# Moving the first loads, sums and norms of a fused attention and feed-forward kernel between queues and places

## The chip, the cores and the metric

The kernel runs on one core of a Trainium2 chip. The core has five engines with an instruction stream each: TensorE (PE, matmuls; PEld is its loading of weights), VectorE (DVE), ScalarE (ACT), GpSimd (POOL) and SyncE (SP). Engines wait for one another through semaphores; each works off its own stream in order. Sixteen DMA engines move data. SP and ACT give them transfers through hardware queues (q1 and q10 in the profile), POOL through a software queue (q0), which can also convert types on the way. The metric is the device time of one execution in microseconds (us). The median of three runs before the change is 415.71 us (415.38 to 417.54).

## What is computed

Attention by cosine similarity over 8 batches of 12 heads, 448 tokens, 64 columns a head, and then a feed-forward layer over the 3584 tokens of all batches, all arrays float32:

```python
q_n = q / (np.linalg.norm(q, axis=-1, keepdims=True) + 1e-06)
k_n = k / (np.linalg.norm(k, axis=-1, keepdims=True) + 1e-06)
scores = np.matmul(q_n, k_n.transpose(0, 1, 3, 2)) / tau        # tau = 0.1
scores = scores - np.max(scores, axis=-1, keepdims=True)
attn = np.exp(scores)
attn = attn / (np.sum(attn, axis=-1, keepdims=True) + 1e-09)
x = np.matmul(attn, v)              # to (3584, 768), heads side by side
h = x @ w_in                        # 768 x 2048
out = np.maximum(0.01 * h, h) @ w_out   # 2048 x 768
```

## The kernel before

Heads go in pairs: a *slot* s is one pair of one batch, six slots to a batch (0 to 5 are the first batch), 48 in all. The 448 tokens of a head are three times 128 tokens (the *main* part) and 64 more (the *remainder*). Two slots make a *group* j (j = 0, 1, 2 for the first batch), whose products with v are taken together.

For each slot the steps are these. `load_first` (slots 0 to 5, line 124) or `load_qk` (from 6 on, line 139) brings q and k; the remainders of q and k of a slot share one row of the tile and are transfers of their own. `squares` (line 175) squares both on POOL (slots 0 and 1 on ACT and DVE). `sums` (line 188) adds them on DVE, in two parts. `roots` (line 199) takes the root on ACT as Exp of half a Ln. `normalise` (line 209) divides on DVE and gives qn. `transposes` (line 245) gives qkT: for slots 0 to 9 on TensorE, with a copy out of PSUM by DVE, from slot 10 on by a DMA transpose that SP issues (line 251). `scores` (line 261) multiplies, and ACT takes Exp (line 288). For a group, `totals` (line 323) sums the weights, `products` (line 335, matmuls at line 316) multiplies with v_b and v_rem, the main part and the remainder of v, and `scale` (line 346, DVE) writes xT. Then `first` (line 365, matmuls at line 374) multiplies xT with w_in, and `two_groups` (line 432, matmuls at line 453) with w_out.

The weights come as bfloat16 through POOL's queue: w_in in four transfers (`load_w_in(0)` to `(3)`, 768 KB each in bfloat16), w_out in five. `load_w_in(0)` and `(1)` are the first half of the columns, even and odd rows. `load_v(j)` brings v_b of a group, 192 KB, by the same queue, and `load_v_rem(b)` the remainders of a batch in four small ones. POOL must issue all these between its squares. `hold` (line 508) is a one-element copy on POOL that makes POOL wait until a given value exists.

The order on each engine is that of the program, written out by hand. Ahead of the loop stand the first loads (lines 471 to 478), slot 0, and the beginnings of slot 1 (lines 517 to 550). The loop over the six first slots (line 553) is staged: turn s takes the scores of slot s, norm s+1 with its transposes, sums s+2 and squares s+3, and every second turn the products of a group two slots back. A transfer of SP waits until the one eight places back on the hardware queues has landed.

After the loop come the products of group 2 (`attend(NQ - 1)`, line 702) and the first feed-forward stage of the first batch. From there each batch has the same turn: `visit` (scores of the next batch between the matmuls of w_out, line 677), `attend_batch` (totals and products, line 648), and `firsts` (the matmuls of w_in, line 667), which runs functions of a list `between` ahead of its m-th block of columns. `norm(s)` (line 653) is roots, normalise, transposes, a load_qk of a later slot, hold and squares of slot s+2. `visit` begins with two score tiles that need qkT of the first four slots of the next batch, so of slots 12 to 15 in the visit that ends the turn `b == 0`.

These lines carry the staging of the loop:

```python
scores(s, (1,))
fill(2)                      # matmuls on a constant tile
if s and n:
    sums(n, (0,))            # n = s + 2
if s < 5:
    normalise(s + 1)
```

Of the kernel before, what the change touches and what calls it, by code (L numbers as in the profile page):

```python
# [16 lines left out]
def kernel(  # L17
# [49 lines left out]
    gp = nc.gpsimd  # L67
# [36 lines left out]
    def load_w_in(i):  # L104
        n0, e = i // 2 * (D_ff // 2), i % 2
        gp.dma_start(
            out=w_in_sb[:, e::2, n0 : n0 + D_ff // 2], in_=w_in_r[e, :, :, n0 : n0 + D_ff // 2]
        )
# [15 lines left out]
    def load_first(eng, x, part, s0, n):  # L124

        h0, i = 2 * s0, 0 if x is q else 1
        if part == 0:
            dst = raw0[:, s0 : s0 + n, :, 4 * i : 4 * i + 3]
            eng.dma_start(
                out=dst.rearrange("p s h t d -> p (s h) t d"), in_=main(x, 0, h0, 2 * n)  # L130
            )
        else:
            dst = raw0[64 * i : 64 * i + 64, s0 : s0 + n, :, 3]
            eng.dma_start(
                out=dst.rearrange("p s h d -> p (s h) d"),
                in_=x[0, h0 : h0 + 2 * n, MAIN:S].rearrange("h p d -> p h d"),
            )

    def load_qk(s):
        if s >= NSLOT:  # L140
            return
        b, h0 = s // NPAIR, 2 * (s % NPAIR)
        both = ldp.tile([128, 2, 7, D], F32, name="qk")
        nc.sync.dma_start(out=both[:, :, 0:3], in_=main(q, b, h0, 2))
        nc.sync.dma_start(out=both[:, :, 4:7], in_=main(k, b, h0, 2))
        for i, x in enumerate((q, k)):
            nc.sync.dma_start(
                out=both[64 * i : 64 * i + 64, :, 3],
                in_=x[b, h0 : h0 + 2, MAIN:S].rearrange("h p d -> p h d"),
            )  # L150
        raw[s] = (both[:, :, 0:4], both[:, :, 4:7])
# [5 lines left out]
    def load_v(j):  # L157
        if j >= B * NQ:
            return
        b, jj = divmod(j, NQ)  # L160
        vb[j] = vbp.tile([128, 4, 3, D], BF16, name="v_b")
        gp.dma_start(out=vb[j], in_=main(v, b, 4 * jj, 4))  # L162

    def load_v_rem(b, parts=slice(0, 4)):
        if b >= B:
            return
        x = vrb[b % 2].rearrange("p j g d -> p (j g) d")
        for lo, h0, h1 in ((0, 0, 2), (64, 2, 6), (0, 6, 10), (64, 10, 12))[parts]:
            gp.dma_start(  # L169
                out=x[lo : lo + 64, h0:h1], in_=v[b, h0:h1, MAIN:S].rearrange("h p d -> p h d")  # L170
            )
# [16 lines left out]
    def sums(s, parts=(0, 1)):  # L188
        if s >= NSLOT:
            return  # L190
        if s not in ss:
            ss[s] = smp.tile([128, 14], F32, name="ss")
        for i in parts:
            o = ss[s][:, 0:8] if i == 0 else ss[s][:, 8:14]
            nc.vector.tensor_reduce(  # L195
                o.rearrange("p (h t) -> p h t", h=2), sqs[s][i], axis=AX.X, op=ALU.add
            )

    def roots(s):
        if s >= NSLOT:  # L200
            return
        nc.scalar.activation(ss[s], ss[s], func=AF.Ln, bias=tiny)
        nc.scalar.activation(ss[s], ss[s], func=AF.Exp, scale=0.5)  # L203
        if s < 2:
            nc.scalar.activation(ss[s], ss[s], func=AF.Identity, bias=eps)
# [55 lines left out]
    def scores(s, kis):  # L261
        key_tiles([(s, ki) for ki in kis])
# [210 lines left out]
        load_first(nc.scalar, k, part, 0, 1)  # L473
    load_first(nc.sync, q, 0, 1, 1)
    load_first(nc.scalar, k, 0, 1, 1)
    for part, s, n in ((1, 1, 1), (0, 2, 1), (0, 3, 1), (0, 4, 2)):
        for x in (q, k):
            load_first(nc.sync, x, part, s, n)
    tiny = cpool.tile([128, 1], F32, name="tiny")
# [28 lines left out]
    def hold(x):  # L508
        seen = smp.tile([128, 1], F32, name="seen")
        gp.tensor_copy(out=seen, in_=x)  # L510

    hold(raw0[:, 0, 0, 3, 0:1])
    for x in (q, k):
        load_first(gp, x, 1, 2, 4)
    load_v_rem(0, slice(0, 2))


    (q_h, k_h), (q_h1, k_h1) = raw[0], raw[1]
# [14 lines left out]
    nc.scalar.activation(sqs[1][0], q_h1, func=AF.Square)  # L533
    normalise(0)
    load_qk(6)
    hold(qn[0][:, 6, 0, 0:1])
    squares(2)
    load_w_in(0)
    load_v(0)
    dst = qtp.tile([128, 7, 128], BF16, name="qkT")  # L540
    qkT[0] = dst.rearrange("p t c -> p (t c)")
    for lo, hi, copy in ((0, 4, nc.scalar.copy), (4, 7, nc.vector.tensor_copy)):
# [4 lines left out]
        copy(out=dst[:, lo:hi], in_=tp[:, lo:hi])  # L547
    fill(3)
    sums(1, (0,))
    roots(1)  # L550


    for s in range(NPAIR):
        j = s // 2 - 1 if s >= 2 else None
        even = s % 2 == 0
        n = s + 2 if s + 2 < NPAIR else None
        if s != 3 and s != 5:
            scores(s, (0,))
        if s == 1:
            roots(2)  # L560
        if j is not None and not even:
            products(j, 1)
        scores(s, (1,))
        fill(2)
        if s and n:
            sums(n, (0,))
        if s < 5:
            normalise(s + 1)
            if s != 1 and s < 4:
                load_qk(s + 7 - (s > 1))  # L570
        if j is not None and not even:
            scale(j, 0)
        if s < 5:
            hold(qn[s + 1][:, 6, 0, 0:1])
            squares(s + 3)
        if s == 0:
            load_v_rem(0, slice(2, 4))
        if s in (1, 2):
            load_w_in(s)
        if s < 2:  # L580
            load_v(s + 1)
        elif s == 2:
            load_w_in(3)
        elif s == 3:
            load_w_out(0)
        elif s == 4:
            load_w_out(1, 4)
        if n:
            sums(n, (1,))
        scores(s, (2,))  # L590
        if s == 5:

            scale(j, 1)
            for m in range(SOON):
                pms[0, m] = banks(1, (0, m, 0), 4 + m)
            first(0, 0, range(KT - 2))
        elif not even:
            fill(2)
        if not even:
            scores(s, (3,))  # L600
        if s < 5:
            transposes(s + 1)
        if s == 0:
            sums(2, (0,))
        if s == 5:
            first(0, 1, range(KT - 2))
            sums(6)
            sums(7)
        elif not even:
            fill(2)  # L610
        if n and s:
            roots(n)
        if j is not None and not even and s < 5:
            scale(j, 1)
        if j is not None and even:
            totals(j)
            scores(s + 1, (0,))
            products(j, 0)

    def attend(j, behind=()):  # L620
        totals(j)
        po = banks(2)
        for e in range(2):
            products(j, e, po[:, e])
        for fn in behind:
            fn()
        for e in range(2):
            scale(j, e)
# [17 lines left out]
                scale(j, e)  # L646

    def attend_batch(b):
        attend_two(b * NQ)
        attend(b * NQ + 2)  # L650


# [64 lines left out]
    for b in range(B):  # L717
        tokens = chunk_cols(b)[1] // 128
        if b == B - 1:
            for ts in range(tokens):  # L720
                for half in range(2):
                    second(b, ts, half)
            break
        order = [((ts, 0), (ts, 1)) for ts in range(tokens)]
        if b == 0:
            order = [((0, 0), (1, 0)), ((2, 0), (0, 1)), ((1, 1), (2, 1))]
        visit(b, order, tokens - 1, three if tokens == 3 else four)
        ready += tokens - 1
        attend_batch(b + 1)
        for j in range((b + 2) * NQ, (b + 3) * NQ):  # L730
            load_v(j)
        load_v_rem(b + 2)
        s = ready
        between = {0: [lambda s=s: norm(s)], 1: [lambda s=s: sums(s + 1)]}
        if b == 0:
            between = {
                0: [lambda: load_qk(14), lambda: load_qk(15), lambda: sums(12)],
                1: [lambda: norm(12), lambda: sums(13)], 4: [lambda: norm(13), lambda: sums(14)],
                7: [lambda: norm(14), lambda: sums(15)], 9: [lambda: norm(15)],
                13: [lambda: sums(16)],  # L740
            }
            ready += 4
        elif tokens == 3:
            between.update({
                4: [lambda s=s: norm(s + 1), lambda s=s: sums(s + 2)],
                7: [lambda s=s: norm(s + 2), lambda s=s: sums(s + 3)],
                10: [lambda s=s: norm(s + 3)], 13: [lambda s=s: sums(s + 4)],
            })
            ready += 4
        else:  # L750
            between.update({
                4: [lambda s=s: norm(s + 1)], 5: [lambda s=s: sums(s + 2)],
                8: [lambda s=s: norm(s + 2)], 12: [lambda s=s: sums(s + 3)],
            })
            ready += 3
        firsts(b + 1, 0, between)
# [35 lines left out]
```

## Time and profile before

| | |
|---|---|
| median of three runs | 415.71 us |
| the profiled execution: its time, its span | 416.25 us, 414.5 us |
| busy: PE, ACT, DVE, POOL | 400.8, 260.2, 191.6, 140.4 us |
| moved by DMA | 54.21 MB |
| DMA queues, share of 16 engines | q1 42.3%, q0 22.8% |
| PE L374 (w_in), PE L453 (w_out) | 147.3, 142.7 us |
| PE L316 (totals and products with v) | 32.0 us |

A row of the timeline reads: start and busy time in us, engine, line, operation, the tile written and the tile read, their shapes, how many in a row, and in brackets how long the engine stood idle before and what ended that. A row of waits has the total time, how often, and the longest. In the DMA answers a row names the transfer and the issuing queue, the size, and the time from issue to landing. Rows of windows have, after the stretch and its length, the busy time of PE, PEld, DVE, ACT and POOL with their instructions, the granted clock of TensorE (1.00 is full), the share of DMA time and GB/s. Landing times that the text gives are the issue plus the time to landing.

### The profile page before, as it was taken

How to read it: one execution, taken by the hardware profiler on the slowest of the kernel's cores; microseconds unless marked ns; L12 is line 12 of the kernel's file. 1: busy time of each engine (PE TensorE's matmuls, PEld its weight loads, DVE VectorE, ACT ScalarE, POOL GpSimd, SP SyncE). 2: the span in 40 equal slices, each digit the busy share in tenths (PEclk: the TensorE clock that was granted, in tenths of full speed). 3: DMA queues.
4: the chain of work that ended last, by engine and by line, in shares of the span. 5: the costliest groups of instructions: out<-in, count | busy, mean ns of one | idle time of the engine just before them, and what ended most of it. 6: DMA issues, size and time to landing. Idle time of an engine off the chain costs nothing.

```text
span 414.5 us, 10095 instructions
## 1 busy us (share of the span) xinstructions
PE 400.8 (97%) x4088; PEld 213.3 (51%) x4099; DVE 191.6 (46%) x412; ACT 260.2 (63%) x448; POOL 140.4 (34%) x214
## 2 busy tenths in 40 slices
PE   8589999999899999999999999999999999999996
PEld 3134655544455555544555555544555565544564
DVE  5575863366453625257261735156362554140021
ACT  4688579745785469745775559855776559934300
POOL 3794453535140624055231533153232530000000
PEclk9899999999999999999999999999999999999999
DMA  6999999686585956476476875576377853210023
GB/s 177 243 213 207 214 159 210 170 150 144 132 183 109 131 138 141 128 113 131 96 188 132 108 174 111 121 115 151 89 180 155 110 90 61 63 40 2 0 76 78
DMA packets 103871, 54.21 MB, mean 131 GB/s; under 512 B 69712, under 2 KB 98768, under 8 KB 103824
## 3 DMA queue, kind: packets, MB, share of 16 engines
q1 hardware_dynamic: 77776, 40.98, 42.3%
q0 software_dynamic: 25200, 12.06, 22.8%
q8 instruction: 32, 0.52, 0.6%
q10 hardware_dynamic: 848, 0.52, 0.4%
q14 instruction: 15, 0.12, 0.1%
HBM read 45.61 MB, written 11.01 MB: 137 GB/s over the span
## 4 chain that ended last, share of the span: by engine, by line
PE 92%; DMA 3%; POOL 2%; issue 1%; ACT 1%; DVE 0%; POOLq 0%
PE ps L374 35%; PE ps L453 30%; PE ps L316 12%; PE ps L276 8%; PE ps L411 5%; PE ps L303 1%; DMA raw<-in_q_dram 1%; POOL sq L184 1%; DMA raw<-in_k_dram 1%; DMA qkT<-qn 1%; ACT pe L288 1%; PE ps L233 1%; POOL v_rem L169 0%; DVE qn L219 0%; POOL v_b L162 0%
## 5 line engine op out<-in xcount | busy, mean ns | idle before, releaser
L374 PE MATMUL ps<-xT,w_in_sb 128*128 128x384 bf16 (+1 forms) x760 | 147.3, 352 | 0.4
L453 PE MATMUL ps<-w_out_sb,hT 64*128 64x384 bf16 x1536 | 142.7, 323 | 0.0
L288 ACT ACTIVATE pe<-ps 128x896 bf16<-128x896 f32 x144 | 123.6, 918 | 23.1 <-PE ps L276 21.1
L381 ACT ACTIVATE hT<-ps 128x384 bf16<-128x384 f32 (+1 forms) x128 | 67.5, 543 | 70.5 <-PE ps L374 70.0
L374 PEld LDWEIGHTS <-w_in_sb 128*128 128x128 bf16 x768 | 74.1, 98 | 71.3 <-issue 3.4
L453 PEld LDWEIGHTS <-hT 64*128 64x128 bf16 x1536 | 73.6, 94 | 54.8 <-issue 3.2
L184 POOL TENSOR_TENSOR sq<-qk 128x512 f32<-128x512 f32 x84 | 77.2, 939 | 13.8 <-DMA qk<-in_k_dram 12.6
L276 PE MATMUL ps<-qkT 64*128 64x448 bf16 (+1 forms) x384 | 54.6, 357 | 6.5 <-DVE qkT L257 3.5
L463 DVE COPY osb<-ps 128x384 f32<-128x384 f32 x48 | 24.5, 552 | 78.0 <-PE ps L453 44.9
L195 DVE TENSOR_REDUCE ss<-sq 128x6 f32<-128x384 f32 (+1 forms) x95 | 54.5, 610 | 4.6 <-POOL sq L184 4.4
L510 POOL CAST seen<-qn 128x1 f32<-128x1 bf16 x48 | 9.1, 189 | 130.1 <-DVE qn L219 123.9
L219 DVE TENSOR_TENSOR qn<-qk,r 128x512 bf16<-128x512 f32 x84 | 49.8, 634 | 2.0 <-DMA qk<-in_k_dram 0.3
L214 DVE TENSOR_SCALAR ss<-ss 128x14 f32<-128x14 f32 x46 | 9.3, 202 | 66.0 <-ACT ss L203 66.0
L351 DVE TENSOR_TENSOR xT<-ps,rb 128x448 bf16<-128x448 f32 x48 | 27.7, 619 | 23.4 <-ACT rb L330 23.3
L162 POOL DMA_DIRECT2D v_b<-in_v_dram x24 | 18.5, 773 | 59.1 <-PE ps L316 59.1
L316 PE MATMUL ps<-pe,v_b 128*32 128x448 bf16 x576 | 32.0, 353 | 0.0
L276 PEld LDWEIGHTS <-qkT 64*128 64x128 bf16 (+1 forms) x384 | 16.6, 97 | 27.5 <-issue 11.0
L329 ACT ACTIVATE rb<-ps 128x448 f32<-128x448 f32 x24 | 13.0, 540 | 23.3 <-PE ps L316 23.3
L288 ACT ACTIVATE pr<-ps 128x896 bf16<-128x896 f32 x24 | 21.4, 921 | 0.6 <-PE ps L276 0.5
L417 DVE COPY osb<-ps 128x384 f32<-128x384 f32 (+1 forms) x9 | 4.6, 512 | 36.6 <-issue 22.6
L316 PEld LDWEIGHTS <-v_b 128*32 128x32 bf16 x576 | 15.3, 97 | 11.9 <-DMA v_b<-in_v_dram 0.3
L411 PE MATMUL ps<-w_out_sb,hT 128*128 128x384 bf16 (+1 forms) x144 | 21.0, 308 | 0.0
(51 smaller groups left out, 196.7 us busy)
## 6 DMA issues: line engine op xcount, KB each, us to landing
qk<-in_q_dram SPq DMA_DIRECT2D x42, 192.0 KB, 3.1
qk<-in_k_dram SPq DMA_DIRECT2D x42, 192.0 KB, 3.1
out_dram<-osb SPq DMA_DIRECT2D x30, 192.0 KB, 3.0
v_b<-in_v_dram POOLq DMA_DIRECT2D x24, 192.0 KB, 4.8
out_dram<-osb SPq DMA_DIRECT2D x12, 384.0 KB, 2.7
w_in_sb<-in_moe_w_in_dram POOLq DMA_DIRECT2D x4, 768.0 KB, 11.8
w_out_sb<-in_moe_w_out_dram POOLq DMA_DIRECT2D x1, 1536.0 KB, 21.7
w_out_sb<-in_moe_w_out_dram POOLq DMA_DIRECT2D x4, 384.0 KB, 22.6
```

Source lines behind the costliest of these rows:

```text
L184: eng.tensor_tensor(sq, x, x, op=ALU.mult)
L195: nc.vector.tensor_reduce(o.rearrange("p (h t) -> p h t", h=2), sqs[s][i], axis=AX.X, op=ALU.add)
L219: nc.vector.tensor_tensor(qn[s][:, lo:hi], x.rearrange("p h t d -> p t h d"), r[:, r0 : r0 + 2 * nt].rearrange("p (h t) -> p t h", h=2) .u ...
L276: nc.tensor.matmul(out=out[:, a, :S], lhsT=x[rows, c0:c1], rhs=x[rows, 0:S], start=True, stop=True,)
L288: nc.scalar.activation(out=dst, in_=sc[:, :, :S], func=AF.Exp, scale=inv_tau)
L316: nc.tensor.matmul(out=x[32 * g : 32 * g + 32, :S], lhsT=weights(g, ki) if ki < 3 else rem(g), rhs=pe[s][:, ki, a, :] if ki < 3 else pr[j] ...
L351: nc.vector.tensor_tensor(xT[m][:, 2 * jj + e, half * S : (half + 1) * S], pos.pop((j, e))[:, :S], rbs[j], op=ALU.mult,)
L374: nc.tensor.matmul(out=pm[:, :n], lhsT=w_in_sb[:, kt, m * 128 : (m + 1) * 128], rhs=xT[c // 2][:, kt, c0 : c0 + n], start=(kt == 0), stop= ...
L381: nc.scalar.activation(out=hT[c][:, m, :n], in_=pms.pop((c, m))[:, :n], func=AF.Prelu, alpha=0.01)
L411: nc.tensor.matmul(out=po2[:, :n], lhsT=hT[c][:, m, ts * 128 : (ts + 1) * 128], rhs=w_out_sb[:, m, lo : lo + n], start=(m == 0), stop=(m = ...
L453: last[i] = nc.tensor.matmul(out=po2[:, i, :HALF], lhsT=hT[c][rows, m, ts * 128 : (ts + 1) * 128], rhs=w_out_sb[rows, m, half * HALF : (ha ...
L463: nc.vector.tensor_copy(out=osb[c, ts][:, half * HALF : (half + 1) * HALF], in_=po2[:, i, :HALF])
```

## The change

SP's transfers of the remainders of slot 1 take slots 1 and 2 in one, POOL's take slots 3 to 5 where they took 2 to 5. The first two v_rem transfers move on POOL from ahead of the squares of slot 2 to behind them, after `load_v(0)`; the other two from turn 0 to turn 1. `load_w_in(0)` moves ahead of the squares of slot 2, the other three one turn up each (turns 0, 1, 2), and `load_v(2)` moves from turn 1 to turn 2, behind `load_w_in(3)`. So v_b(2) is now sent for after all four transfers of w_in. The first part of the sums of slot 2 moves on DVE from the end of turn 0 to ahead of the norm of slot 1, and the roots of slot 2 on ACT from turn 1 to the end of turn 0. In the turn `b == 0`, loads 14 and 15 and sums 12 move into `attend_batch(1)`, ahead of its products, norm 12 between the products of the second and the third group, and sums 13 to 15 and norms 13 to 15 each move to the place in `between` that the one before had.

```diff
-    for part, s, n in ((1, 1, 1), (0, 2, 1), (0, 3, 1), (0, 4, 2)):
+    for part, s, n in ((1, 1, 2), (0, 2, 1), (0, 3, 1), (0, 4, 2)):
         for x in (q, k):
             load_first(nc.sync, x, part, s, n)
...
     hold(raw0[:, 0, 0, 3, 0:1])
     for x in (q, k):
-        load_first(gp, x, 1, 2, 4)
-    load_v_rem(0, slice(0, 2))
+        load_first(gp, x, 1, 3, 3)
...
     normalise(0)
     load_qk(6)
+    load_w_in(0)
     hold(qn[0][:, 6, 0, 0:1])
     squares(2)
-    load_w_in(0)
     load_v(0)
+    load_v_rem(0, slice(0, 2))
...
     sums(1, (0,))
+    sums(2, (0,))
     roots(1)
...
-        if s == 1:
-            roots(2)
...
-        if s == 0:
-            load_v_rem(0, slice(2, 4))
-        if s in (1, 2):
-            load_w_in(s)
-        if s < 2:
-            load_v(s + 1)
-        elif s == 2:
-            load_w_in(3)
+        if s < 3:
+            if s == 1:
+                load_v_rem(0, slice(2, 4))
+            load_w_in(s + 1)
+            if s != 1:
+                load_v(s // 2 + 1)
         elif s == 3:
...
-        if s == 0:
-            sums(2, (0,))
...
-        if n and s:
+        if n:
             roots(n)
...
     def attend_batch(b):
+        if b == 1:
+            load_qk(14)
+            load_qk(15)
+            sums(12)
         attend_two(b * NQ)
+        if b == 1:
+            norm(12)
         attend(b * NQ + 2)
...
-                0: [lambda: load_qk(14), lambda: load_qk(15), lambda: sums(12)],
-                1: [lambda: norm(12), lambda: sums(13)], 4: [lambda: norm(13), lambda: sums(14)],
-                7: [lambda: norm(14), lambda: sums(15)], 9: [lambda: norm(15)],
+                0: [lambda: sums(13)], 1: [lambda: norm(13), lambda: sums(14)],
+                4: [lambda: norm(14), lambda: sums(15)], 7: [lambda: norm(15)],
                 13: [lambda: sums(16)],
```

## The prediction

> **What bounds the kernel now.** First the page: how full TensorE is, and when the DMA engines are full.
>
> ```profile
> span 414.5 us, 10095 instructions
> PE 400.8 (97%) x4088; PEld 213.3 (51%) x4099; DVE 191.6 (46%) x412; ACT 260.2 (63%) x448; POOL 140.4 (34%) x214
> ...
> DMA  6999999686585956476476875576377853210023
> ```
>
> PE is idle for 13.7 us only (414.5 - 400.8). The DMA digits, one per 10.4 us, stay at 9 from the second to the seventh: until about 60 us the DMA engines are a second limit. Then the waits of PE, over the first 60 us and over the whole run: two are a matter for this change.
>
> ```profile
> PE ps L276 <- DVE qkT L257: 3.5, 2, 3.2
> ...
> PE ps L276 <- DMA qkT<-qn: 1.1, 1, 1.1
> ```
>
> The timeline shows where the first, 3.2 us, comes from, and the later point that decides my forecast.
>
> ```profile
> 12.98 1.82 POOL L184 TENSOR_TENSOR sq<-raw 128x512 f32<-128x512 f32 x2 [3.77 <-issue]
> 14.84 0.55 DVE L195 TENSOR_REDUCE ss<-sq 128x6 f32<-128x384 f32 x1 [2.43 <-POOL sq L184]
> 15.31 0.61 DVE L257 COPY qkT<-ps 128x896 bf16<-128x896 bf16 x1
> 15.98 0.93 PE L276 MATMUL ps<-qkT 64*128 64x448 bf16 x4 [3.17 <-DVE qkT L257]
> ...
> 39.10 0.74 PE L316 MATMUL ps<-pe,v_b 128*32 128x448 bf16 x12
> ```
>
> POOL's squares of slot 2 stand 3.77 us ("issue" hides a DMA: the k remainders that POOL sent for at 7.06 land 5.8 us later, at 12.86). DVE's sums wait for them, the copy of qkT(1) stands behind these sums in DVE's order, and PE behind the copy. The row at 39.10 is the first product with v_b(2). From there PE has no wait of length but one until the end. So a change before 39.10 is worth what it moves that row by, and no more.
>
> Last, the DMA answers: three weight and value loads (issued at 22.20, 23.01 and 26.62), and the packets of each queue from 26 to 29 us.
>
> ```profile
> w_in_sb<-in_moe_w_in_dram POOLq DMA_DIRECT2D x1, 768.0 KB, 11.2
> v_b<-in_v_dram POOLq DMA_DIRECT2D x1, 192.0 KB, 11.5
> ...
> w_in_sb<-in_moe_w_in_dram POOLq DMA_DIRECT2D x1, 768.0 KB, 15.3
> ...
> q0 software_dynamic: 523, 0.40, 83.6%
> q1 hardware_dynamic: 523, 0.26, 42.1%
> ```
>
> So w_in(1) lands at 33.4, v_b(2) at 34.5 and w_in(3) at 41.9; w_in(2), issued at 25.83, takes 12.3 and lands at 38.1. POOL's queue (q0) lands in its order, and against SP's queue (q1) it gets packet for packet.
>
> **The change, part by part**, on the profiled execution (span 414.5 us, 416.25 with what lies around it; the median of the runs, 415.71, is 0.54 below that).
>
> *Remainders by SP.* SP's two transfers of 32 KB for slot 1 become two of 64 KB for slots 1 and 2. They landed at 7.1 and 7.25 (issued 2.68 and 3.35, 4.4 and 3.9 us). 128 more packets each, at the 400 per us that q1 makes alone (737 in 12 to 14 us, beside a quarter of another queue's time), put 0.3 to 0.6 us on them. ACT's L533, started at 7.47, waits that long, but its reader on DVE starts at 9.33, 1.25 us after its end: cost 0, and 1:1 beyond 1.2 us. The loads behind them on SP wait for the landing of earlier ones anyway (1.6 us idle before 6.68).
>
> *POOL's head.* Two v_rem issues (1.28 us) go behind the squares of slot 2, a w_in issue (0.81) comes in. The hold on qn(0), freed at 8.62, ends near 8.9 (9.22 before), and the squares of slot 2 now need only SP's transfers, the last of them landed at 8.54: they start at about 9.0 instead of 12.98. The first half is done at 10.0.
>
> *Sums of slot 2 moved up.* DVE's 0.69 us fall into its gap of 0.96 us before 10.97: 10.01 to 10.7, with 0.27 to spare. If the squares come later than that, norm 1 and all behind it go 1:1. The second half (0.55) follows norm 1 at 12.4, the copy of qkT(1) ends at 13.6, and PE starts slot 1 at 13.65: 2.3 us sooner.
>
> *Roots of slot 2 moved up.* ACT's 0.51 us go from behind the first Exp of slot 1 (17.39) to behind the last of slot 0 (13.36), where ACT stood 3.22 us: cost 0.
>
> *w_in(0) sent for at 7.8 instead of 14.75.* Its first packets move at about 9.6 and meet the loads of slots 3 to 5, of which the k parts landed at 12.8 and 15.3. w_in(0) has 384 packets (128 partitions, 3 rows each); alone a w_in takes 3.8 us (41.9 - 38.1), with a q1 packet between each two 0.95 more. The six loads are 1,536 packets of 768 B (1,152 KB), of which I estimate 150 moved by then. So slot 3 lands near 14.9 (some 350 packets between as many of w_in, 4.3 us, and 1 for the landing). For the rest q1 needs 8.4 us from 9.6 on: w_in(0) 3.8, v_b(0) 1.1, and 1,390 packets of its own at 400 per us. Slots 4 and 5 land near 19. POOL's squares of slot 4 started at 20.43; they now find their data at 19 instead of being free to start at 16.4. Of the 2.3 us some 1.0 to 1.7 are left at slot 3; I take 1.2. The bounds are 0 (nothing gained) and 2.3.
>
> *v_b(2) behind all four w_in.* Before, POOL's order was w_in(1), v_b(2), w_in(2), w_in(3); now v_b(2) comes last, and PE wants it at 39.10 - 1.2 = 37.9. When does it land? Upper bound: the same bytes were down at 41.9, when w_in(3) landed. Lower: from 9.6 on, four w_in at 3.8, three v_b at 1.1 (34.5 - 33.4) and 0.7 for v_rem make 19.2 us if q1 got nothing, so 29 to 30. With one q1 packet for each of their 3,840 (4x384, 3x512, 768), at 400 per us, 9.6 us more: 38.4, and about 1 until it counts as landed, 39.4. The same sum for w_in(3) before, with all 4,450 packets that q1 then had left (1,390 and 768 for each of slots 6 to 9), gives 40.9 where the trace has 41.9. I add that 1.0 to 39.4 and take 40.5 (the start at 9.6 is itself an estimate), with 39.3 to 41.9 as the range, nearer the upper end because the trace shows no free DMA time between 10 and 40 us. PE's products then start at 40.5, not at 39.10: **+1.4 us**, whatever the start gained. The wait shows as 2.6 us on DMA v_b.
>
> The Trainium skill speaks against an early w_in as well: "DMA: Bandwidth & Descriptors", section "Issuing engines are not separate DMA queues", says that transfers of all issuing engines share the same 16 DMA engines, so that a second queue saves issue time alone. By that rule v_b(2) is late; were the queues independent it would land near 30, and the fast rival below would hold. The 523 packets on each queue agree with the rule.
>
> *Norms 12 to 15 sooner.* The other wait, with its cause:
>
> ```profile
> 102.50 1.26 SPq L251 DMA_TRANSPOSE qkT<-qn  x1
> ...
> 105.52 0.38 PE L276 MATMUL ps<-qkT 64*64 64x448 bf16 x4 [1.06 <-DMA qkT<-qn]
> ```
>
> qn(15) is ready at 100.2, SP still issues loads of slot 18 until 102.4, and the transpose takes 2.98 us from 102.50. Each norm moves one place up, norm 15 to where norm 14 stood, whose transpose went out at 98.65: landed by 101.7, before PE asks at 104.46. **-1.06 us**. What it adds in front: sums 12 (1.14) in DVE's gap of 1.50 before 79.48; roots 12 (0.5) on ACT between 80.47 and 81.87, where it waits 1.40; norm 12 (1.57) on DVE from 81.77, which puts scale 5 from 83.05 to 83.4; its xT is read after twelve matmuls that begin at 83.26 and last 2.6 us, so 0 (cover 1.3 us). POOL's squares 14 (1.82) go ahead of the loads of v_b(6) to (8), read first near 131. SP's loads of slots 14 and 15 keep their places at 78.47 and 81.56.
>
> Sum: +1.4 - 1.06 = +0.3 on 416.25, so 416.6 for a profiled run and 416.1 against the median.
>
> **The rivals.**
>
> (a) *v_b(2) in time*: q1 is held back more than packet for packet while w_in flows (in 18 to 19 us it moved nothing, though loads were out), and v_b(2) lands before 37.9. Then the start keeps 1.2 (up to 2.3): 415.71 - 1.06 - 1.2 = 413.4, down to 412.4. Against it: loads held back are those of slots 3 to 5, which shrinks that same gain.
>
> (b) *PE's clock drops in the wait*, slower. After the 3.2 us wait at 12.8 the trace grants half the clock:
>
> ```profile
> 16.00:17.00 1.00, 0.91 (x4) 0.24 (x6) 0.52 (x1) 0.42 (x1) 1.00 (x3) 0.50 1.20 271
> 18.00:19.00 1.00, 1.00 (x4) 0.13 (x2) 0.93 (x4) 1.00 (x2) 1.00 (x3) 0.50 1.05 182
> ```
>
> Some 3.4 us at 0.50 (the mean of 15 to 16 is 0.82, of 19 to 20 0.97). There PE had room; at 40.5 it is the limit, and 3.4 us at half speed cost up to 1.7: 417.8. It decides once the wait nears 3 us, so with a v_b(2) landing after 41, or a start that keeps more; the wait of 1.06 us at 104 dropped nothing. "TensorE: Matmul & The Clock Gate" of the Trainium skill, Part 1, gives an idle window of about 3.4 us that runs freely, so the same wait may or may not be hit; the trace's 3.4 us agree.
>
> (c) *Slots 3 to 5 starve*, slower: w_in(0) holds their loads beyond 24 us, the squares of slot 4 start 4 us after 20.43, and the chain reaches the products at 42 to 43, after v_b(2). That is 2.9 to 3.9 - 1.06 on 415.71, 417.6 to 418.6. Against it stand the 8.4 us above: 5 us more would have to be lost.
>
> **How the numbers follow.** Forecast 0.50, (a) 0.17, (b) 0.20, (c) 0.13. 0.5% (2.1 us) is about what a measurement of this kernel can tell from no change. The forecast with its landing from 39.3 to 41.9 gives 415.0 to 417.6, so no change. Of (a) 0.11 lies below 413.6; of (b) 0.10, of (c) 0.08 and of late landings 0.03 above 417.8. That makes 0.11 faster, 0.68 same, 0.21 slower. The range leaves out the better half of (a) and the worst of (b) and (c): 413.6 to 418.4. Predicted is 416.1.
>
> **What would show it.** Right: POOL's squares of slot 2 near 9.0 with no long wait; PE's slot 1 near 13.7; squares of slot 4 waiting for DMA raw; a wait of PE at L316 on DMA v_b of 2 to 3 us that ends at 40 to 41; no PE wait on DMA qkT near 104. Wrong: no such wait at L316 (then a), PEclk at 0.50 after it (b), or PE's waits in slots 2 to 4 longer than before (c). If q1's packets in 10 to 20 us are far from one for one with q0's, my landing time is wrong, and with it the sum.

## The result, and the profile after

The changed kernel takes 418.91 us (median of 14 runs, 416.71 to 421.36), the kernel before 416.16 in the runs beside it (14 runs, 415.38 to 417.88). The ratio is 1.0054 (95% interval 1.0032 to 1.0076): slower by about half a per cent. By the ratio that is 2.3 us; the two medians lie 2.75 apart. Forecast were 416.1 and no change, and 418.91 is above the forecast range's end of 418.4. The profiled execution took 419.46 us, against 416.25.

First the page: the span, and the busy time of each engine.

```profile
span 417.7 us, 10096 instructions
PE 401.8 (96%) x4088; PEld 213.5 (51%) x4099; DVE 193.5 (46%) x412; ACT 259.7 (62%) x448; POOL 140.3 (34%) x214
```

The span grew by 3.2 us. PE is idle for 15.9 us (13.7 before) and busy for 1.0 longer, although it ran the same 4088 matmuls: some of them were slower. The waits of PE (in all, times, longest) show which stall went and which came:

```profile
PE ps L316 <- DMA v_b<-in_v_dram: 5.2, 1, 5.2
...
PE ps L276 <- DVE qkT L257: 0.7, 1, 0.7
```

The 3.2 us on qkT are down to 0.7 and the 1.1 us on the transposes are gone. In their place stands one wait of 5.2 us for v_b(2). The timeline (start, duration, engine, line, operation, and in brackets the idle time before it with its releaser) has the rows that the prediction named:

```profile
9.08 1.82 POOL L184 TENSOR_TENSOR sq<-raw 128x512 f32<-128x512 f32 x2
13.77 0.55 PE L276 MATMUL ps<-qkT 64*128 64x448 bf16 x4 [0.72 <-DVE qkT L257]
18.68 0.83 POOL L184 TENSOR_TENSOR sq<-raw 128x384 f32<-128x384 f32 x1 [0.97 <-DMA raw<-in_k_dram]
35.01 0.75 PE L316 MATMUL ps<-pe,ones 128*32 128x448 bf16 x12
41.19 1.31 PE L316 MATMUL ps<-pe,v_b 128*32 128x448 bf16 x12 [5.24 <-DMA v_b<-in_v_dram]
61.13 0.57 PE L276 MATMUL ps<-qkT 64*64 64x448 bf16 x8
108.52 0.57 PE L276 MATMUL ps<-qkT 64*64 64x448 bf16 x8
```

Of the kernel before, two rows are needed beside these, the totals of group 2 and the score tiles that open the turns of the second part:

```profile
38.34 0.75 PE L316 MATMUL ps<-pe,ones 128*32 128x448 bf16 x12
56.69 0.57 PE L276 MATMUL ps<-qkT 64*64 64x448 bf16 x8
```

The start is faster. PE reaches the totals of group 2 (35.01) 3.33 us sooner than before (38.34), but the first product with v_b(2) starts 2.09 later, at 41.19 against 39.10, and takes 1.31 us for twelve matmuls where it took 0.74. The table by stages says why (stretch, its length, busy time of PE, PEld, DVE, ACT, POOL, then the granted clock, the DMA share and GB/s):

```profile
38.00:40.00 2.00, 0.00 (x0) 0.00 (x0) 0.00 (x0) 0.04 (x1) 0.00 (x0) 0.81 1.37 205
40.00:42.00 2.00, 0.81 (x12) 0.38 (x16) 0.00 (x0) 0.00 (x0) 0.00 (x0) 0.50 1.32 203
...
44.00:46.00 2.00, 2.00 (x10) 0.86 (x7) 1.51 (x4) 0.00 (x0) 0.00 (x0) 0.50 1.32 205
46.00:48.00 2.00, 2.00 (x14) 1.17 (x13) 1.93 (x6) 1.00 (x3) 0.88 (x2) 0.98 1.32 203
```

The clock falls to half inside the wait, at 39.3, and is back only at 46.1. PE, full from 41.19 on, runs 4.9 us of that at half speed. Between the first product and the score tiles (row 61.13) lie 19.94 us; before, the same work took 17.59 (39.10 to 56.69). That is 2.35 us for the clock. Last the queue: v_b(2), sent for at 24.18, and the packets of both queues from 33 to 36 us (packets, MB, share of the time of 16 engines).

```profile
v_b<-in_v_dram POOLq DMA_DIRECT2D x1, 192.0 KB, 17.0
...
q0 software_dynamic: 244, 0.49, 86.0%
q1 hardware_dynamic: 249, 0.15, 22.7%
```

v_b(2) takes 17.0 us (11.5 before) behind w_in(2) and w_in(3) in POOL's queue (q0), which gets one packet for each one of SP's queue (q1). In the same 3 us of the kernel before, SP's queue moved nothing and POOL's 352 packets. The account of the profiled execution: products later by 2.09, clock 2.35, and from the score tiles at 61.13 to the end of those at 108.52 47.96 us instead of 49.21, so -1.25. The sum is +3.19, against 3.2 measured. (The three parts follow one another from 39.10 to the end of the score tiles, so they must add up to the shift of these; that the spans differ by as much says that nothing was gained or lost after them.)

The same kernel profiled a second time (419.66 us, span 417.9) ends alike and gets there in another way. Expected were the q part of slots 4 and 5 at about 13 or at 18 to 19, their k part at 18 to 21 and v_b(2) at 41 to 42.5.

```profile
20.14 0.83 POOL L184 TENSOR_TENSOR sq<-raw 128x384 f32<-128x384 f32 x1 [1.66 <-DMA raw<-in_k_dram]
37.46 0.75 PE L316 MATMUL ps<-pe,ones 128*32 128x448 bf16 x12
42.11 1.20 PE L316 MATMUL ps<-pe,v_b 128*32 128x448 bf16 x12 [3.71 <-DMA v_b<-in_v_dram]
61.34 0.57 PE L276 MATMUL ps<-qkT 64*64 64x448 bf16 x8
```

Here the start gained 0.88 us, not 3.33. The q part of slots 4 and 5 landed at 17.3 (12.8 in the first profile), the k part at 20.1, v_b(2) at 42.05. What differs is which was sent for first: in the first profile SP issued that q load at 7.90 and POOL w_in(0) at 7.96, in the second w_in(0) went at 7.67 and q at 7.70. The three other profiles with an early w_in(0) (e1, e4 and e10 below) have w_in(0) first too, and there the q load took 10.0 to 10.8 us, as here 9.6, and not 4.9. The products are 3.01 later than before and the clock costs 1.64 (19.23 against 17.59).

### The profile page after: what moved, and what is told of

It reads as the page before. It is cut to its first block, busy times and chain, and to the rows that moved or that the text cites. A ratio compares the mean times of both kernels' runs of the same rounds, so it can differ in the third digit from the quotient of the medians.

```text
span 417.7 us, 10096 instructions
## 1 busy us (share of the span) xinstructions
PE 401.8 (96%) x4088; PEld 213.5 (51%) x4099; DVE 193.5 (46%) x412; ACT 259.7 (62%) x448; POOL 140.3 (34%) x214
## 4 chain that ended last, share of the span: by engine, by line
PE 89%; DMA 8%; POOL 1%; SPq 1%; issue 0%; DVE 0%
PE ps L374 35%; PE ps L453 30%; PE ps L316 10%; PE ps L276 7%; PE ps L411 5%; DMA v_b<-in_v_dram 4%; DMA raw<-in_k_dram 2%; DMA raw<-in_q_dram 1%; PE ps L303 1%; POOL sq L184 1%; SPq L129 0%; PE ps L233 0%; POOL w_in_sb L106 0%; POOL v_rem L169 0%; SPq L134 0%
## 5 line engine op out<-in xcount | busy, mean ns | idle before, releaser
L276 PE MATMUL ps<-qkT 64*128 64x448 bf16 (+1 forms) x384 | 53.9, 354 | 3.2 <-ACT pe L288 1.9
L219 DVE TENSOR_TENSOR qn<-qk,r 128x512 bf16<-128x512 f32 x84 | 50.7, 645 | 2.0 <-DVE r L215 0.6
L316 PE MATMUL ps<-pe,v_b 128*32 128x448 bf16 x576 | 33.1, 362 | 5.2 <-DMA v_b<-in_v_dram 5.2
L162 POOL DMA_DIRECT2D v_b<-in_v_dram x24 | 18.6, 777 | 54.5 <-PE ps L316 54.5
L276 PEld LDWEIGHTS <-qkT 64*128 64x128 bf16 (+1 forms) x384 | 16.7, 96 | 23.2 <-issue 10.1
L417 DVE COPY osb<-ps 128x384 f32<-128x384 f32 (+1 forms) x9 | 4.6, 513 | 36.6 <-issue 22.6
```

The costliest lines, as they stand in the source:

```text
L219: nc.vector.tensor_tensor(qn[s][:, lo:hi], x.rearrange("p h t d -> p t h d"), r[:, r0 : r0 + 2 * nt].rearrange("p (h t) -> p t h", h=2) .u ...
L276: nc.tensor.matmul(out=out[:, a, :S], lhsT=x[rows, c0:c1], rhs=x[rows, 0:S], start=True, stop=True,)
L316: nc.tensor.matmul(out=x[32 * g : 32 * g + 32, :S], lhsT=weights(g, ki) if ki < 3 else rem(g), rhs=pe[s][:, ki, a, :] if ki < 3 else pr[j] ...
```

## The experiments

The theory after the result: the loss is the place of v_b(2), last in POOL's queue. It makes PE wait, so nothing that the start gains can be used, and the wait brings the clock down as a second price. The rivals: that w_in sent for before the squares of slot 2 is at fault (it starves slots 3 to 5 and shifts the whole queue), and that a late v_b(2) alone, without the clock, explains the time.

### v_b(2) ahead of w_in(2) again (e1)

```diff
         if s < 3:
             if s == 1:
+                load_v(2)
                 load_v_rem(0, slice(2, 4))
             load_w_in(s + 1)
-            if s != 1:
-                load_v(s // 2 + 1)
+            if s == 0:
+                load_v(1)
```

> The changed kernel with one load put back: v_b(2) is sent for in turn 1, ahead of w_in(2), and no longer behind w_in(3). Theory (the order of v_b(2) on POOL's queue makes the loss): with w_in(1) and v_b(1) ahead of it, v_b(2) lands near 31, before PE asks at 35.9; the wait of 5.24 us at L316 and the half clock behind it go, the start keeps its 3.3 us (totals at 35.01 where they were at 38.34) and the second wait's 1.06. 416.2 - 3.3 - 1.1 = 411.8. Rival (the early w_in(0), or the start's other moves, make the loss): PE waits elsewhere, for raw, w_in or qk, and the time is 416 to 419.

Measured: 414.16 us, 0.9952 (0.9933 to 0.9972). The timeline of its profile, an execution of 416.15 us, near the slow end of its ten (413.11 to 416.27):

```profile
21.24 1.18 POOL L184 TENSOR_TENSOR sq<-raw 128x384 f32<-128x384 f32 x1 [1.31 <-DMA raw<-in_k_dram]
39.47 0.75 PE L316 MATMUL ps<-pe,ones 128*32 128x448 bf16 x12
40.24 0.74 PE L316 MATMUL ps<-pe,v_b 128*32 128x448 bf16 x12
```

This one place turns +0.54% into -0.48%: a kernel with all the rest of the change is faster than before. v_b(2) lands at 30.8, PE no longer waits for it, and from the products to the tiles at 57.82 it needs 17.58 us, the full-clock figure. But I expected 411.8. The start of this profile gained nothing (totals at 39.47, 38.34 before): slots 4 and 5 landed at 18.75 (q) and 21.16 (k), against 13.91 and 15.32 before, POOL's squares of slot 4 waited for them, and the clock was at half from 24.0 to 27.4. So w_in sent for early seems to have a price of its own, which e5 and e6 look at.

### v_b(2) late in the kernel before (e2)

```diff
-        if s < 2:
-            load_v(s + 1)
+        if s == 0:
+            load_v(1)
         elif s == 2:
             load_w_in(3)
+            load_v(2)
```

> The kernel before with that load alone moved: v_b(2) behind w_in(3) in turn 2, nothing else. Theory: the bytes ahead of it are those that ended at 41.9, so v_b(2) lands at 41 to 42, PE waits 2 to 3 us at L316 where it had no wait, and if the wait holds an idle clock window up to 1.7 to 2.4 us more are lost: 418.5 to 421, slower. Rival (v_b(2) is late in the changed kernel because of the early w_in(0) and not by its place): 416.2, no wait at L316.

Measured: 419.39 us, 1.0066 (1.004 to 1.0092). The timeline, and two rows of the stages (same columns as above):

```profile
43.00 1.15 PE L316 MATMUL ps<-pe,v_b 128*32 128x448 bf16 x12 [1.94 <-DMA v_b<-in_v_dram]
62.23 0.57 PE L276 MATMUL ps<-qkT 64*64 64x448 bf16 x8
...
39.81:43.22 3.41, 1.47 (x27) 0.48 (x28) 0.20 (x1) 2.54 (x7) 0.00 (x0) 1.00 1.35 197
43.22:46.63 3.41, 3.41 (x35) 1.33 (x28) 1.20 (x3) 0.00 (x0) 0.00 (x0) 0.50 1.32 206
```

The same loss, with nothing else of the change: the cause can be put into the old kernel by moving one call. And the clock fell after a wait of only 1.94 us, and cost 1.65 (19.23 from the products to the tiles, against 17.58 at full clock). That speaks against my "decides once the wait nears 3 us". (The profiled execution, 421.09 us, is the slowest of the four; its start was late besides, with the totals at 40.12.)

### Only the norms and sums of slots 12 to 15 sooner (e3)

The edit is the `attend_batch` and `between` part of the change's diff, on the kernel before.

> The kernel before with the second part of the change alone: norms 12 to 15 one place sooner. Theory: the transpose of slot 15 lands near 101.6, the PE wait of 1.06 us on DMA qkT near 104 goes and none takes its place: 415.1, 0.26% less. Rival (another engine, ACT or DVE, ends the same wait, or norm 12 ahead of the products delays the first matmuls of w_in): 416.2 or more, with a PE wait at L276 or L374 between 80 and 106.

Measured: 415.16 us, 0.997 (0.9958 to 0.9983), a gain of 1.2 to 1.3 us. The wait at L276 on the transposes is gone. This part is worth what it was costed at.

### The wait filled with matmuls that compute nothing used (e4, e10)

```diff
         po = banks(2)
+        if j == NQ - 1:
+            fill(23)
         for e in range(2):
             products(j, e, po[:, e])
```

> The changed kernel with 23 matmuls on the constant tile (23 x 0.215 = 4.9 us) between the totals and the products of group 2, where PE waits for v_b(2). They compute nothing that is used. Theory (the wait costs 2.1 us by itself and the dropped clock 2.3 more): v_b(2) still lands near 41, PE's products start there, but PEclk stays 1.00: 416.2 + 2.1 - 1.06 = 417.2, against 418.9 without them. Rival (the clock costs nothing, another thing holds the products after 41): 418.9 as without them; or, if the fill delays the products, more.

Measured: 418.05 us, 1.0058 (1.0033 to 1.0082), against 1.0054 without the fill: no gain in time. In its profile the clock stays full through the products, and these need 17.60 us to the tiles; but the start was late in that execution (totals at 38.77), the products began behind the fill at 44.70, and v_b(2) had landed at 42.24. 23 were too many, so a second kernel has `fill(16)`:

> The changed kernel with 16 matmuls on the constant tile (3.4 us) ahead of the products of group 2, seven less than before, so that they end ahead of v_b(2) when the start is quick. They compute nothing that is used. Theory (part of the loss is the dropped clock): the wait at L316 shrinks to some 2 us or less, the landing stays at 40 to 42, PEclk stays 1.00 after it, and the stretch from the products to the next visit is 17.6 us and not 19.9: 1 to 2 us less than the changed kernel, 417 to 418. Rival (the clock makes no difference): 418.9.

Measured: 417.87 us, 1.0034 (1.0014 to 1.0054). Its timeline:

```profile
41.72 0.76 PE L316 MATMUL ps<-pe,v_b 128*32 128x448 bf16 x12
59.32 0.57 PE L276 MATMUL ps<-qkT 64*64 64x448 bf16 x8
```

Twelve products in 0.76 us instead of 1.31, and 17.60 us to the tiles instead of 19.94 or 19.23. So the 1.64 to 2.35 us are the price of PE's idling: keep it busy, and they are gone. The fill loses part of that again, as it ended 0.8 us after v_b(2)'s landing at 40.93. The median is 1.0 us below the changed kernel's, but the intervals of the two ratios overlap, so the clock's price rests on the traces more than on the times.

### w_in(0) behind the squares of slot 2 again (e5, e6)

In both, `load_w_in(0)` stands behind `squares(2)` once more. e5 has v_b(2) early as in e1, e6 leaves it last.

```diff
     load_qk(6)
-    load_w_in(0)
     hold(qn[0][:, 6, 0, 0:1])
     squares(2)
+    load_w_in(0)
     load_v(0)
```

> The changed kernel with two loads put back: v_b(2) ahead of w_in(2), as in the run before this, and w_in(0) behind the squares of slot 2, where it stood before the change. Theory (the early w_in(0) catches the loads of slots 4 and 5: in three profiles their k part landed at 18.6 to 21.2 where it was 15.3): with w_in(0) issued at 10.8 and moving from 12.6 these loads land near 15 to 17, the squares of slot 4 wait under 1 us, PE keeps its clock in the start, the totals of group 2 begin near 35 to 36, and the time is 416.5 - 3.0 - 1.1 = 412.4 or less. Rival (the early w_in(0) is needed, or the start does not depend on it): 414.2, as with v_b(2) alone put back.

Measured: 413.43 us, 0.9926 (0.9911 to 0.9941). The totals stand at 36.77, 1.6 us before those of the kernel before; slots 4 and 5 land at 13.18 and 14.29, where e1 had 18.75 and 21.16. The expectation was a microsecond too good. Until 22.42 POOL waited 1.78 us for the landing of an earlier v_b before it issued w_in(2).

> The changed kernel with w_in(0) put back behind the squares of slot 2 and v_b(2) left behind w_in(3). Theory (the place of v_b(2) alone sets the end): v_b(2) lands at 41 to 43 as in the changed kernel, PE waits 5 to 6 us at L316, the clock drops for part of what follows: 418 to 420, no better than the changed kernel's 418.9. Rival (v_b(2) is late because w_in(0) went early): it lands before 38 and the time is 413 to 415.

Measured: 417.89 us, 1.0033 (1.0017 to 1.005). Its timeline and two rows of its stages:

```profile
40.26 0.75 PE L316 MATMUL ps<-pe,v_b 128*32 128x448 bf16 x12 [2.90 <-DMA v_b<-in_v_dram]
57.86 0.57 PE L276 MATMUL ps<-qkT 64*64 64x448 bf16 x8
...
35.33:38.74 3.41, 2.03 (x25) 0.76 (x24) 0.99 (x2) 2.51 (x5) 0.18 (x1) 1.00 1.20 205
38.74:42.15 3.41, 1.89 (x34) 0.96 (x35) 0.76 (x2) 0.65 (x4) 0.00 (x0) 1.00 1.35 204
```

v_b(2) still lands at 40.25 and PE still waits, so the late landing does not come from the early w_in(0); its place behind the last w_in is enough. This execution, the fastest of its ten, is also the one that my forecast described, though in another kernel: a wait of 2.90 us, the clock kept, and a span of 414.4, 0.1 below that of before. Of the ten runs the three with a mean granted clock of 0.999 or more took 416.2 to 416.7 us, the seven below 417.5 to 419.5. So the same kernel seems to be hit by the clock in some executions and not in others. The mean clock does not say at which place it was low, and only one execution was profiled, so the split of the runs fits the theory without proving it.

What brings the clock down can be read from all the profiles together. The clock changes only at fixed steps: its changes within a profile lie whole multiples of 3.413 us apart (15.91 and 43.22 in e2, eight steps; 21.80 and 42.28 in the second profile of the changed kernel, six). So they give the edges of windows of that length for the whole profile, also where nothing changed. In e6 the clock falls once, at 414.21 behind the last matmul; 110 steps of 3.4133 back lies an edge at 38.74, inside the wait from 37.36 to 40.26. (Ten steps further back, at 4.61, the warm-up matmuls begin to come twice as often, which agrees.) The two rows above are the windows on either side of 38.74. PE's idle time in a window is its length less PE's busy time:

| profile | window | PE idle (us) | clock in the next window |
|---|---|---|---|
| changed kernel, first | 35.85 to 39.26 | 3.31 | half |
| changed kernel, first | 39.26 to 42.68 | 1.93 | half |
| e2 | 39.81 to 43.22 | 1.94 | half |
| e1 | 10.30 to 13.71 | 1.56 | half |
| e6 | 35.33 to 38.74 | 1.38 | full |
| e6 | 38.74 to 42.15 | 1.52 | full |

Divided so from the first edge on, the 13 profiles keep one rule: the 15 windows with 1.56 us of idle time or more are each followed by half clock, all others, with 1.52 or less, by the full one. (In e5 and e9, where the clock never falls, the edges come from the warm-up matmuls alone.) PE's busy times are modelled, so the limit itself is good to a few hundredths at best.

### The start alone (e7, e8)

e8 is the kernel before with the remainder transfers of the change, and the first two v_rem behind `load_v(0)`; e7 has besides the sums and roots of slot 2 sooner.

```diff
-    for part, s, n in ((1, 1, 1), (0, 2, 1), (0, 3, 1), (0, 4, 2)):
+    for part, s, n in ((1, 1, 2), (0, 2, 1), (0, 3, 1), (0, 4, 2)):
...
-        load_first(gp, x, 1, 2, 4)
-    load_v_rem(0, slice(0, 2))
+        load_first(gp, x, 1, 3, 3)
...
     load_v(0)
+    load_v_rem(0, slice(0, 2))
```

> The kernel before with the start's moves alone: remainders of slots 1 and 2 by SP, of 3 to 5 by POOL, the first v_rem behind v_b(0), sums and roots of slot 2 sooner; all w_in, v_b(1), v_b(2) and the norms 12 to 15 as before. Theory: POOL's squares of slot 2 begin near 9.0, PE starts slot 1 near 13.7 and the totals of group 2 near 35.5 (38.34 before); 416.5 - 2.8 = 413.7. Rival (the gain is lost before the products, to later loads or to ACT): 415.5 to 416.5.

> The kernel before with the transfers of the remainders alone (SP slots 1 and 2, POOL 3 to 5, the first v_rem behind v_b(0)); the sums and roots of slot 2 stay where they were. Theory: the copy of qkT(1) no longer waits, PE starts slot 1 near 13.7, but the roots of slot 2 stand behind the first Exp of slot 1, so slot 2 gains about 0.5 to 1 us less than with all of the start's moves: 414.2 to 414.7. Rival (the gain is made by the sums and roots, and the squares were no limit): 416.2.

Measured: e7 414.00 us, 0.9937 (0.9922 to 0.9952); e8 413.99 us, 0.9936 (0.9921 to 0.9951). From the timeline of e8:

```profile
8.77 1.82 POOL L184 TENSOR_TENSOR sq<-raw 128x512 f32<-128x512 f32 x2
36.59 0.74 PE L316 MATMUL ps<-pe,v_b 128*32 128x448 bf16 x12
102.99 0.38 PE L276 MATMUL ps<-qkT 64*64 64x448 bf16 x4 [1.03 <-DMA qkT<-qn]
```

The remainders, with the two v_rem transfers, are the whole gain of the start, 2.7 us. v_b(2) lands at 32.66, before PE asks at 36.6, and the products move up by 2.5. The sums and roots, which I had expected to be worth some tenths to a microsecond, are worth nothing. The wait for the transposes is still there.

### Remainders and norms together (e9)

The edits of e8 and e3 on the kernel before.

> The kernel before with the two parts that gained: the transfers of the remainders, and norms 12 to 15 one place sooner; all w_in and v_b and the sums and roots of slot 2 as before. Theory (the two gains lie in different places and add): 414.0 - 1.1 = 412.9, with no PE wait at L276 near 102 and none at L316; less than with either alone and less than the 413.4 of the changed kernel with w_in(0) and v_b(2) put back. Rival (they overlap, or the second wait is replaced): 413.5 to 414.

Measured: 412.70 us (412.24 to 413.06), 0.9898 (0.9867 to 0.993). From its timeline:

```profile
37.15 0.74 PE L316 MATMUL ps<-pe,v_b 128*32 128x448 bf16 x12
```

The gains add: 0.9936 times 0.997 is 0.9906. This half of the change beats both kernels, by 1.0% and 1.5%.

## Why the prediction was wrong

| part | forecast (us) | measured |
|---|---|---|
| products with v_b(2) later | +1.4 | +2.09, +3.01 (two profiles) |
| half clock after the wait | 0 (rival b: up to 1.7) | +2.35, +1.64 |
| norms 12 to 15 | -1.06 | -1.25, -1.2 (traces); -0.30% alone |
| sum in the profile | +0.3 | +3.2, +3.4 |

*The step that failed is the cost of the wait to PE's clock, taken as 0.* The place, the wait and its cause were forecast; the wait was priced by its landing alone, and the clock was left to rival (b), whose bound of 1.7 us for 3.4 us at half speed is what e2 (1.65) and the second profile (1.64) show. In the first profile the clock stayed down for two such stretches, of which PE was working through 4.9 us, hence 2.35. Two things made (b) look less likely than it was. The wait was sized at 2.6 us and came out at 5.24 and 3.71. And the condition "once the wait nears 3 us" was wrong in itself: 1.94 us was enough in e2, and 2.90 was not in the profile of e6. What counts is how the idle time falls into a window: 1.5 us in one of 3.41 is the limit. By that even the forecast's own wait of 2.6 us stays free only if an edge lies within a quarter of a microsecond of its middle, some 0.5 of 3.41 us: an estimate of one case in seven, if the edge is as likely anywhere, where the prediction gave (b) 0.20 in all. "TensorE: Matmul & The Clock Gate" of the Trainium skill, Part 1, gives such a free-running window of about 3.4 us; the half-clock stretches of 3.4 and 6.8 us agree. The prediction quoted it and then used a threshold on the length of the wait all the same.

The second step that failed is *v_b(2)'s landing*; in the second profile it cost as much as the clock (1.6 us of products later than forecast, and 1.64). It was put at 40.5 (39.3 to 41.9). It came at 41.18 and 42.05, and at 40.25 to 42.24 in e4, e6 and e10. The packet-for-packet sum was right in kind and 0.7 to 1.5 us low in the changed kernel, which makes the +1.4 a +2.1 to +3.0. The sign that the prediction named for this showed in part: in 10 to 20 us SP's queue moved 1761 packets and POOL's 1295 (1629 and 1228 in the second profile); from 20 to 33 us it was one for one, 1847 and 1853. Over 10 to 40 us SP's queue was 304 and 245 packets ahead; at the prediction's 400 per us that is 0.8 and 0.6 us, an estimate, and the rest is not explained. The sum's 1 us until a landing and 0.7 us for v_rem rest on no row.

*The gain of the start* was taken as 1.2 with bounds of 0 and 2.3. The two profiles have 3.33 and 0.88, the one beyond the upper bound, the other near the forecast: a few hundredths of a microsecond decide anew in each execution whether q or w_in(0) is sent for first. "Whatever the start gained" held within the changed kernel, where an earlier start only made the wait longer. It is not general: between e2 and e6, which differ in when POOL sends for v_b(2) (28.67 and 24.25), the landing moves by 2.7 us.

*Rival (c)* did not come about: slots 4 and 5 were late (k part at 18.6 and 20.1, forecast 19), but PE was at the totals before v_b(2) in both profiles. A milder form is likely: e1 against e5 has w_in(0) early and late with v_b(2) in time, 0.9952 against 0.9926, some 1.1 us by the ratios, but these intervals overlap, so it is not shown. *Rival (a)* fell with the landing, but its consequence is what e1 and e5 show: with v_b(2) in time the change is faster.

*Right*: the squares of slot 2 at 9.08 (9.0), slot 1 on PE at 13.77 (13.65), the squares of slot 4 waiting for DMA raw, the remainder transfers at no cost, the transposes' wait gone, and the norms' gain, -1.25 against -1.06. The sums and roots of slot 2 were costed at nothing, and e7 against e8 agrees. Two readings were a little off and change nothing: the DMA digits of 9 reach to 72.5 us, not 60, and landings from 39.3 to 41.9 give 414.9 to 417.5 by the prediction's own sum.

What stays open: what share of the median's 2.3 us is the clock and what the landing, since only single executions were profiled and the times of e4 and e10 do not part from those of the changed kernel; and whether sending q first is enough for it to land first, as one profile alone has it so.

## What to carry to other kernels

Where a transfer is moved to the end of a queue, work out its landing and compare it with when its reader asks; every gain ahead of that reader is then worth nothing, and one moved call (e1) can hide or show all of it. A wait of TensorE at full load has two prices, its length and up to 1.7 us for each stretch at half clock behind it, so any wait above some 1.5 us has to be priced at both, with the chance that 1.5 us of it fall into one window of 3.41. Take a change of several parts apart before it is kept or dropped: here the remainders and the norms were worth -1.0% together, and the new places of w_in and v_b(2) turned that into +0.5%.

## What the runs showed of the hardware that was not expected

- A wait of 1.94 us lowered the clock (e2), one of 2.90 (e6) did not, and with the wait filled by unused matmuls (e10) it stayed full. In e6 an edge at 38.74 cuts the wait into 1.38 and 1.52 us; in e2 all of it lies in one window. Idle time of 1.56 us or more in a window of 3.41 was enough in every case on record, also when it came in several pieces (e1, 10.30 to 13.71).
- One kernel has two orders of landing: the q part of slots 4 and 5 came at 12.8 us where it was sent for 0.06 us ahead of w_in(0), and at 17.3 where it was sent for 0.03 us behind. The start gained 3.3 or 0.9 us by it, and the span, 417.7 and 417.9, hardly shows it, since v_b(2) decides.
- In 33 to 36 us the two queues moved 244 and 249 packets, but POOL's, of 2 KB, took 86.0% of the engines' time and SP's, of some 600 bytes (0.15 MB in 249), 22.7%. SP's 83 packets per us compare with some 370 in 12 to 14 us of the kernel before, when POOL's queue took a quarter of the time. Packet for packet is not byte for byte: beside large packets the small ones came far more slowly, though no row shows whether SP's queue had packets waiting all the time.
